# Chunked attention and an MLP block on one core: g broadcast by a product, key transposes in two PSUM banks, fills on GpSimd, other steps for attention

## The chip, the cores and the metric

The kernel runs on one core of a Trainium2 chip. The metric is the device time of one execution in microseconds, median of 11 runs. Engines are named as in the profile: PE is TensorE (matmuls), DVE is VectorE, ACT is ScalarE, POOL is GpSimd, SP is SyncE. SP and POOL issue the DMAs: those that change the type from fp32 to fp16 are on POOL, the stores and the DMA transposes on SP.

## The reference

Two stages follow one another. The first is attention in chunks of 32 queries, each chunk seeing 16 positions to its left, 8 to its right and 8 memory positions; batch 4, 8 heads, 768 positions, head dimension 64:

```
for c in range(nc):                       # chunk of 32 queries
    l_start, r_end = max(0, 32*c - 16), min(S, 32*c + 32 + 8)
    k_full = concat([mem_k, k[:, :, l_start:r_end]])
    v_full = concat([mem_v, v[:, :, l_start:r_end]])
    scores = q_c @ k_full.T / sqrt(D)
    out[:, :, c_start:c_end] = softmax(scores) @ v_full
```

The second is, on x of shape (4, 768, 512), a normalisation and two products with a residual:

```
xn = (x - mu) / sqrt(var + 1e-6) * g_ln
y  = x + relu(xn @ w_ch1) @ w_ch2         # 512 -> 2048 -> 512
```

## The kernel before

**Tiles and units.** The 3072 rows are 24 tiles of 128 rows, six to a batch. Three tiles make a unit, so there are eight units. A unit has 28 steps: steps 0 to 15 are the first product (`up`, one of 16 column blocks per step, four matmuls of 384 columns), steps 16 to 27 the second (`down`, four matmuls of 512 columns per step). The division by the standard deviation is put off to the end: `finish` multiplies by `rstd`, adds x and stores.

**Where attention stands.** Attention for later tiles is spread over these steps. A dictionary `plan`, filled by `at(u, step, fn, ...)`, says which helper is emitted after the product of a step; what is emitted first stands first in the queue of every engine. `attend(i, s0, s1, u)` places one tile: `scores` and the first `soften` at s0, the second at s0 + 1, `values` at s1, `norm` at s1 + 1, `turn_x` and `stats` at s1 + 2. Unit 0 is different: its tiles are attended in a hand-written prologue, with `warm` matmuls on zeros where PE would wait.

**Keys and queries.** A block is 256 positions of k or q. POOL loads it (`load_block`, tile `st`), DVE reorders it (`mix`, `st` to `iv`). For batches 0 and 1 PE transposes it in eight matmuls into PSUM (`turn_block`, L209), and copies bring it to `KT` and `QR`: four `key_piece` copies per key block, alternately on DVE and ACT, and edges from one block to the next (`key_right`, `key_left`). For batches 2 and 3 SP transposes it by DMA (`cross`, L239, `iv` to `rawk` and `QR`), and `spread` copies `rawk` to `KT`. `iv` has four buffers, so the next `mix` waits until a `cross` has read its buffer.

**PSUM.** `att` is two tiles of two banks, `mm` four tiles of one bank; `slot` takes them in turn.

**Fills.** `ones`, `clear_keys` and three memsets put constants into `V` and `KT`, which have two buffers each; `early(1)` does it for batch 1 on DVE at step 15 of unit 0. `v_mem` copies the memory values into `V`, `count_v` corrects the counts in the edge groups. `gb`, g in all 128 partitions, comes by one DMA from POOL.

**The queues.** POOL works in order: loads, then `root` (the standard deviation, waiting on `stats`), then the next loads; batch 3's first loads stand behind the root of tile 11. SP also works in order: `turn_x` of tile 11 is ahead of batch 2's first `cross`.

Of the kernel before, what the change touches and what calls it, by code (L numbers as in the profile page):

```python
# [15 lines left out]
def kernel(  # L16
# [12 lines left out]
    nc = tc.nc  # L29
# [22 lines left out]
    memKT = sb.tile([128, B, 4, 8], FP16, name="memKT")  # L52
    gb = sb.tile([128, 512], FP32, name="gb")
    band = sb.tile([128, 2], FP32, name="band")
    cnt = sb.tile([128, 3], FP32, name="cnt")
# [114 lines left out]

    def key_piece(b, src, g, first, lo, n, eng):

        copy(eng, free(KT[b % 2], GW * g + 16 + 8 * lo, [[W, 4], [8, n], [1, 8]]),
             free(src, 4 * (first + lo), [[1, 4], [4, n], [128, 8]]))

    def key_right(b, g, eng, src=None):

        o = free(KT[b % 2], GW * g + 80, [[W, 4], [1, 8]])
        if src is None:
            copy(eng, o, free(KT[b % 2], GW * (g + 1) + 16, [[W, 4], [1, 8]]))  # L180
        else:
            copy(eng, o, free(src, 0, [[1, 4], [128, 8]]))

# [4 lines left out]

    def keys(b, blk, src, e0, e1):

        g = 4 * blk
        if blk:
            key_right(b, g - 1, e1, src)
        key_piece(b, src, g, 0, 0, 9, e0)
        key_piece(b, src, g + 1, 8, -2, 11, e1)
        key_piece(b, src, g + 2, 16, -2, 11, e0)
        key_piece(b, src, g + 3, 24, -2, 10, e1)
        if blk:
            key_left(b, g, e0)

    def turn_block(b, blk, which, p=None):
        if p is None:
            if (b, blk) not in block_slot:
                block_slot[b, blk] = slot("att")
            p = block_slot[b, blk][:, which, :]
        pv = as16(p)
        i = pick(iv, ("b", b, blk, which))
        for r in range(8):
            nc.tensor.matmul(  # L209
                out=pv[:, 128 * r : 128 * r + 128],  # L210
                lhsT=i[:, 128 * r : 128 * r + 128], rhs=identity,
                is_transpose=True, start=True, stop=True,
            )
        return pv

    block_slot = {}

    def queries(b, blk, pv, e0, e1):
        part_q(b, blk, 0, pv, e0)
        part_q(b, blk, 1, pv, e1)  # L220

    def part_q(b, blk, half, pv, eng):
        copy(eng, free(QR[b % 2], 1024 * blk + 64 * half, [[128, 8], [1, 64]]),
             free(pv, 64 * half, [[128, 8], [1, 64]]))

    def turn_keys(b, blk, e0, e1, *how):
        keys(b, blk, turn_block(b, blk, 0, *how), e0, e1)

    def turn_queries(b, blk, e0, e1, *how):
        queries(b, blk, turn_block(b, blk, 1, *how), e0, e1)  # L230

# [9 lines left out]
    def spread(b, blk, e0, e1):  # L241
        keys(b, blk, pick(rawk, ("b", b, blk)), e0, e1)

# [169 lines left out]

    load_mem_v(0)

    PAIR = 1.0 / 128 + 15.0 / 2**20
# [9 lines left out]

    nc.vector.memset(zero, 0.0)
    ones(0, 0, 2)
    nc.vector.memset(V[0][0:32, 0, :, :], 0.0)
# [4 lines left out]

    load_block(0, 0, 0)
    load_block(0, 0, 1)
    make_identity(nc, identity)

# [5 lines left out]

    total(cnt[:, 0:1], 16, 128)
    total(cnt[:, 1:2], 0, 80)
    total(cnt[:, 2:3], 96, W)
    nc.vector.tensor_tensor(out=cnt[:, 1:2], in0=cnt[:, 1:2], in1=cnt[:, 2:3], op=ALU.add)
    total(band[:, 0:1], 56, 96)
    total(band[:, 1:2], 0, 32)  # L450
    total(cnt[:, 2:3], 88, 96)
    nc.vector.tensor_tensor(out=band[:, 1:2], in0=band[:, 1:2], in1=cnt[:, 2:3], op=ALU.add)
    nc.vector.tensor_scalar(out=band, in0=band, scalar1=NEG, scalar2=None, op0=ALU.mult)

    nc.vector.memset(V[0][64:96, NG - 1, :, :], 0.0)
    load_v(0, 0)
    load_v(0, 1)
    load_block(0, 1, 0)
    nc.gpsimd.dma_start(out=gb, in_=dram(moe_g_ln, 0, [[0, 128], [1, 512]]))
    load_w1(0)  # L460
# [14 lines left out]
    load_v(0, 8)  # L475
    load_v(0, 9)
    load_w2(2)
    load_v(0, 10)
# [6 lines left out]
    mem_vals(0)  # L485
    warm(11)
    mem_keys()
    mem_cols(0, act)
    mix(0, 0, 0, dve)
    pv = turn_block(0, 0, 0, mm[0])  # L490
    key_piece(0, pv, 0, 0, 0, 9, dve)
    key_piece(0, pv, 1, 8, -2, 11, act)
    warm(1)
    mix(0, 0, 1, dve)
    pq = turn_block(0, 0, 1, mm[1])
    part_q(0, 0, 0, pq, act)
    key_piece(0, pv, 2, 16, -2, 11, dve)
    part_q(0, 0, 1, pq, dve)
    warm(1)
    v_mem(0, 0, 2, dve)  # L500
    count_v(0, 0, 0)
    scores(0, 0)
    soften(0, 0, 0)
    soften(0, 0, 1)
    key_piece(0, pv, 3, 24, -2, 10, act)
    warm(2)
    mix(0, 1, 0, dve)
    pv = turn_block(0, 1, 0, mm[2])
    key_right(0, 3, act, pv)
    values(0, 0)  # L510
# [3 lines left out]
    soften(0, 1, 1)  # L514
    ones(0, 2, NG)
    key_piece(0, pv, 4, 0, 0, 9, dve)
    v_mem(0, 2, 6, dve)
    key_piece(0, pv, 5, 8, -2, 11, act)
    warm(2)
    turn_x(0, 0)  # L520
    warm(1)
    up_tile(0, 0, 0, act)
    values(0, 1)
    norm(0, 1)
    key_left(0, 4, dve)
    key_piece(0, pv, 6, 16, -2, 11, dve)
    key_piece(0, pv, 7, 24, -2, 10, act)
    warm(4)
    turn_x(0, 1)
    warm(1)  # L530
    up_tile(0, 0, 1, dve)
    up_tile(0, 1, 0, act)
    up_tile(0, 1, 1, dve)
    mix(0, 1, 1, dve)
    turn_queries(0, 1, dve, act, mm[0])
    warm(1)
    scores(0, 2)
    soften(0, 2, 0)
    soften(0, 2, 1)
    up_tile(0, 2, 0, dve)  # L540
    values(0, 2)
    norm(0, 2)
    up_tile(0, 2, 1, act)
    turn_x(0, 2)
    up_tile(0, 0, 2, dve)
    up_tile(0, 1, 2, act)
    up_tile(0, 2, 2, dve)
    for t in range(3):
        stats(0, t)
    def early(i):  # L550
        ones(i, 0, NG)
        nc.vector.memset(V[i][0:32, 0, :, :], 0.0)
        nc.vector.memset(V[i][64:96, NG - 1, :, :], 0.0)
        clear_keys(i, dve)
        count_v(i, 0, 0)
        count_v(i, 1, NG - 1)

# [17 lines left out]
    for t in range(3):  # L575
        at(0, 16 + t, root, 0, t)
    at(0, 14, v_mem, 0, 6, NG, dve)
    at(0, 14, count_v, 0, 1, NG - 1)
    at(0, 15, early, 1)
    for b in range(1, B):  # L580
        at(0, 14, load_mem_v, b)
        at(0, 23 + b, mem_vals, b)
    at(0, 15, mix, 0, 2, 0, dve)
    at(0, 16, turn_keys, 0, 2, dve, act)
    attend(3, 17, 19, 0)
    at(0, 19, mix, 0, 2, 1, dve)
    at(0, 20, turn_queries, 0, 2, dve, act)
    attend(4, 21, 23, 0)
    attend(5, 22, 24, 0)

# [20 lines left out]
    for b in (1, 2, 3):  # L611
        u = 2 * b - 1
        if b == 1:
            order = [(load_pair, (0,))] + [(load_v, (g,)) for g in range(4)]
            order += [(load_pair, (1,)), (mem_cols, (pool,)), (load_v, (4,)), (load_v, (5,))]
            order += [(load_pair, (2,))] + [(load_v, (g,)) for g in range(6, 12)]
            ahead(1, order, 19, 0.25)
            for blk, s in ((0, (3, 4)), (1, (10, 13)), (2, (24, 25))):
                at(1, s[0] - 1, mix, 1, blk, 0, dve)
                at(1, s[0], turn_keys, 1, blk, dve, act)  # L620
                at(1, s[1] - 1, mix, 1, blk, 1, dve)
                at(1, s[1], turn_queries, 1, blk, act, dve)
            for i in range(3):
                at(1, (4, 12, 19)[i], v_mem, 1, 4 * i, 4 * i + 4, dve)
            attend(6, 5, 9, 1)
            attend(7, 12, 15, 1)
            attend(8, 17, 20, 1)
        else:
            w = u - 1
            at(w, 0, load_pair, b, 0)  # L630
            for i in range(2):
                at(w, 1, load_v, b, i)
            at(w, 2, load_pair, b, 1)
            at(w, 8, mix_pair, b, 0)
            for i in range(2, 4):
                at(w, 9, load_v, b, i)
            at(w, 11, mem_cols, b, pool)
            at(w, 12, mix_pair, b, 1)
            at(w, 13, load_pair, b, 2)
            for i in range(4, 8):  # L640
                at(w, 10 + i, load_v, b, i)
            at(w, 24, mix_pair, b, 2)
            for i in range(8, 12):
                at(w, 13 + i, load_v, b, i)
            at(w, 21, cross_pair, b, 0)
            at(w, 22, cross_pair, b, 1)
            at(u, 3, cross_pair, b, 2)
            at(w, 26, spread, b, 0, dve, act)
            at(w, 27, spread, b, 1, dve, act)
            at(u, 9, spread, b, 2, dve, act)  # L650
            for i in range(3):
                at(w, (17, 20, 23)[i], v_mem, b, 4 * i, 4 * i + 4, dve)
            attend(6 * b, 2, 7, u)
            attend(6 * b + 1, 7, 13, u)
            attend(6 * b + 2, 13, 18, u)
        for i in range(3):
            attend(6 * b + 3 + i, 1 + 6 * i, 6 + 6 * i, u + 1)

# [50 lines left out]
```

## Time and profile before

| | |
|---|---|
| median of 11 runs | 254.59 us (251.08 to 259.15) |
| profiled execution | 257.5 us, span 255.7 us |
| mean granted PE clock | 0.938 |
| PE busy | 221.3 us (87%) |
| DVE busy | 135.0 us (53%) |
| ACT busy | 100.2 us (39%) |
| POOL busy | 96.1 us (38%) |

The span goes from the first to the last instruction; the rest of the profiled execution's time lies around it. In lines of the timeline the columns are start and duration in microseconds, engine, line of the kernel, operation, output and inputs, shapes and count; a bracket at the end gives how long the engine was idle before it and what ended that. In the rows of slices each digit stands for a fortieth of the span, in tenths.

### The profile page before, as it was taken

The page shows a single profiled execution, that of the slowest core. Times are in us where ns is not written, and L with a number is a line of the kernel's source. Part 1 is how long each engine was busy: PE and PEld are TensorE (multiplying, and loading weights), DVE is VectorE, ACT ScalarE, POOL GpSimd, SP SyncE. Part 2 cuts the span into 40 slices and gives each one's busy share as a digit, 9 for nine tenths or more (in the row PEclk, how much of TensorE's full clock was granted, in tenths as well). Part 3 has the DMA queues.
Part 4 walks back from the last instruction along what each step waited for, and adds up shares of the span by engine and source line. Part 5 has one row for each costly group of instructions (what it writes and reads, how often), then busy time and mean ns, then how long its engine had stood idle before and what let it go on. Part 6 is the DMA issues. An engine that isn't in the chain of part 4 may idle for free.

```text
span 255.7 us, 4863 instructions
## 1 busy us (share of the span) xinstructions
PE 221.3 (87%) x1924; PEld 129.9 (51%) x1924; DVE 135.0 (53%) x318; ACT 100.2 (39%) x204; POOL 96.1 (38%) x162
## 2 busy tenths in 40 slices
PE   7578774987798979999238999999999999999994
PEld 2345662443465436654124645664566466546653
DVE  5565456148677644864134843685666426444312
ACT  3521342355356424640216921661478135412300
POOL 8955349996702198129200139532002101110000
PEclk9957998699999999999756999999999999999999
DMA  6999999999961299618995129962963321121012
GB/s 103 146 194 199 200 196 158 154 171 102 183 95 21 64 120 181 60 21 158 132 131 164 23 62 148 173 50 73 204 126 27 81 85 21 23 84 60 3 41 82
DMA packets 72935, 27.59 MB, mean 108 GB/s; under 512 B 60944, under 2 KB 69392, under 8 KB 72912
## 3 DMA queue, kind: packets, MB, share of 16 engines
q0 software_dynamic: 46288, 15.34, 55.2%
q1 hardware_dynamic: 26624, 11.93, 22.1%
q8 instruction: 15, 0.25, 0.4%
q14 instruction: 8, 0.07, 0.1%
HBM read 30.54 MB, written 6.29 MB: 144 GB/s over the span
## 4 chain that ended last, share of the span: by engine, by line
PE 64%; DVE 13%; DMA 10%; issue 3%; ACT 3%; POOL 2%; SPq 2%; DVEq 0%; POOLq 0%; ACTq 0%
PE mm L340 26%; PE mm L366 23%; DMA rawk<-iv 5%; PE att L253 4%; PE att L274 4%; DMA st<-in_k_dram 3%; PE mm L351 3%; DVE xs L282 2%; DVE KT L102 2%; SPq L239 2%; DVE V L102 2%; PE att L209 2%; DVE xn L294 2%; PE mm L388 1%; DMA QR<-iv 1%
## 5 line engine op out<-in xcount | busy, mean ns | idle before, releaser
L340 PE MATMUL mm<-xT,w1c 128*128 128x384 f16 x464 | 84.6, 334 | 5.3 <-DVE rT L334 5.0
L366 PE MATMUL mm<-w2c,rT 128*128 128x512 f16 x368 | 86.0, 386 | 0.0
L340 PEld LDWEIGHTS <-w1c 128*128 128x128 f16 x464 | 51.0, 115 | 29.8 <-issue 8.0
L366 PEld LDWEIGHTS <-rT 128*128 128x128 f16 x368 | 35.1, 99 | 39.6 <-issue 1.9
L332 ACT ACTIVATE rT<-mm 128x384 f16<-128x384 f32 (+1 forms) x62 | 30.5, 495 | 59.9 <-PE mm L340 39.4
L334 DVE TENSOR_SCALAR rT<-mm 128x384 f16<-128x384 f32 (+1 forms) x63 | 35.6, 568 | 30.9 <-PE mm L340 24.0
L305 POOL TENSOR_SCALAR veps<-sq 128x1 f32<-128x1 f32 x24 | 6.9, 286 | 113.0 <-ACT junk L299 112.7
L126 POOL DMA_DIRECT2D V<-in_v_dram x48 | 37.7, 810 | 3.6 <-DMA w2c<-in_moe_w_ch_dram 1.9
L263 ACT ACTIVATE AT<-att,band 104x512 f16<-104x512 f32 x48 | 31.3, 684 | 5.2 <-PE att L253 4.1
L375 DVE SCALAR_TENSOR_TENSOR osb<-mm,rstd,xs 128x512 f32<-128x512 f32 x23 | 17.3, 751 | 26.8 <-PE mm L366 26.8
L299 ACT ACTIVATE junk<-xs,nmean 128x512 f16<-128x512 f32 x24 | 17.2, 718 | 21.5 <-DVE nmean L288 21.4
L253 PE MATMUL att<-QR,KT 64*104 64x64 f16 x384 | 16.3, 237 | 6.2 <-DVE KT L102 5.4
L253 PEld LDWEIGHTS <-KT 64*104 64x104 f16 x384 | 13.3, 138 | 12.5 <-issue 12.2
L100 ACT COPY KT<-rawk 128x352 f16<-128x352 f16 (+2 forms) x16 | 9.4, 651 | 23.3 <-DMA rawk<-iv 23.3
L281 DVE RECIPROCAL rec<-att 128x8 f32<-128x8 f32 x24 | 4.9, 205 | 25.5 <-PE att L274 22.7
L294 DVE SCALAR_TENSOR_TENSOR xn<-xs,nmean,gb 128x512 f16<-128x512 f32 x24 | 17.9, 747 | 0.4
L309 POOL TENSOR_TENSOR rstd<-veps,mhalf 128x1 f32<-128x1 f32 x24 | 16.8, 700 | 2.0
L282 DVE SCALAR_TENSOR_TENSOR xs<-att,rec 128x512 f32<-128x512 f32 x24 | 16.6, 692 | 0.8
L102 DVE COPY iv<-st 128x1024 f16<-128x1024 f16 x24 | 10.2, 440 | 10.4 <-DMA QR<-iv 5.8
L118 POOL DMA_DIRECT2D st<-in_q_dram x24 | 13.6, 581 | 5.4 <-DMA w1c<-in_moe_w_ch_dram 3.7
L118 POOL DMA_DIRECT2D st<-in_k_dram x24 | 13.8, 581 | 3.2 <-DMA w1c<-in_moe_w_ch_dram 2.3
L209 PEld LDWEIGHTS <-iv 128*128 128x128 f16 x96 | 6.2, 105 | 16.8 <-DVE iv L102 16.7
(62 smaller groups left out, 140.0 us busy)
## 6 DMA issues: line engine op xcount, KB each, us to landing
out_dram<-osb SPq DMA_DIRECT2D x23, 256.0 KB, 2.1
V<-in_v_dram POOLq DMA_DIRECT2D x40, 96.0 KB, 5.3
st<-in_k_dram POOLq DMA_DIRECT2D x24, 128.0 KB, 4.8
st<-in_q_dram POOLq DMA_DIRECT2D x24, 128.0 KB, 5.4
w1c<-in_moe_w_ch_dram POOLq DMA_DIRECT2D x4, 512.0 KB, 10.0
w2c<-in_moe_w_ch_dram POOLq DMA_DIRECT2D x4, 512.0 KB, 10.2
V<-in_v_dram POOLq DMA_DIRECT2D x8, 80.0 KB, 5.3
xT<-xn SPq DMA_TRANSPOSE x18, 2.5
```

The lines of the kernel that those rows point to most:

```text
L102: eng.tensor_copy(out=out, in_=in_)
L118: nc.gpsimd.dma_start(out=s[:, 512 * par : 512 * par + 512], in_=dram((k, q)[which], (b * H + 4 * par) * HS + blk * 256 * D, [[512, 32], [ ...
L126: nc.gpsimd.dma_start(out=V[b % 2][lo:hi, g, :, 0:64], in_=dram(v, b * H * HS + (64 * g - 16 + lo) * D, [[64, hi - lo], [HS, H], [1, 64]]),)
L253: nc.tensor.matmul(out=p[0:W, par, (4 * gg + j) * 64 : (4 * gg + j) * 64 + 64], lhsT=KT[b % 2][rows, 2 * t + gg, j, :], rhs=free(QR[b % 2] ...
L263: nc.scalar.activation(out=free(AT[t % 3], 32 * c, [[64, 16], [1, 32]]), in_=free(p, 4 * c, [[64, 16], [1, 4], [8, 8]], W), func=ACTF.Exp, ...
L282: nc.vector.scalar_tensor_tensor(out=x.rearrange("p (h d) -> p h d", h=8), in0=free(p, 0, [[128, 8], [1, 64]]), scalar=1.0, in1=free(r, 0, ...
L294: nc.vector.scalar_tensor_tensor(out=xn[i % 4], in0=xs[i % 9], scalar=nmean[t], in1=gb, op0=ALU.add, op1=ALU.mult,)
L332: nc.scalar.activation(out=o, in_=p, func=ACTF.Relu)
L334: nc.vector.tensor_scalar(out=o, in0=p, scalar1=0.0, scalar2=None, op0=ALU.max)
L340: nc.tensor.matmul(out=p, lhsT=free(w1c[c][:, dt, :], i, [[4, 128]]), rhs=xT[u % 2][:, dt, 128 * lo : 128 * (lo + n)], start=(dt == 0), st ...
L366: nc.tensor.matmul(out=p, lhsT=rT[c][:, k_, 128 * i : 128 * i + 128], rhs=w2c[c][:, k_, :], start=(c == 0 and k_ == 0), stop=(c == 3 and k ...
L375: nc.vector.scalar_tensor_tensor(out=o, in0=p, scalar=rstd[t % 9], in1=xs[t % 9], op0=ALU.mult, op1=ALU.add,)
```

## The change

- g comes as one row of 2 KB on SP (`grow`); a product of a row of ones with it puts it into PSUM in all partitions, and ACT copies it to `gb`.
- Key transposes go into two banks, four matmuls each. `key_piece` takes a half; DVE copies the first bank's half of each piece, ACT the second's. In the prologue the banks are two `mm` tiles, in `turn_keys` the two halves of one `att` tile. The last two pieces are put off (`more_keys`). Queries take a slot of their own and both copies go to ACT.
- `early(1)` moves to POOL and to step 19; other fills, `count_v` and parts of `v_mem` move to other places; the identity is made before the load of q.
- In the prologue the order of copies, ReLUs and tiles changes.
- In unit 1 the steps of keys, queries and attention change. In units 2, 4 and 6 attention starts at steps 0, 5, 10 instead of 1, 7, 13, its values at 5, 10, 15 instead of 6, 12, 18. Of each batch from 2 on the first two blocks' `cross` moves from steps 21 and 22 to 18 and 19, their `spread` from 26 and 27 to 24 and 26.

```diff
-    def key_piece(b, src, g, first, lo, n, eng):
+    def key_piece(b, src, g, first, lo, n, eng, half=None):
+        h, m = (0, 8) if half is None else (4 * half, 4)
+        copy(eng, free(KT[b % 2], GW * g + 16 + 8 * lo + h, [[W, 4], [8, n], [1, m]]),
+             free(src, 4 * (first + lo), [[1, 4], [4, n], [128, m]]))
...
+    PIECES = ((0, 0, 9), (8, -2, 11), (16, -2, 11), (24, -2, 10))
+    def pieces(b, blk, banks, which):
+        for k_ in which:
+            for half, eng in ((0, dve), (1, act)):
+                key_piece(b, banks[half], 4 * blk + k_, *PIECES[k_], eng, half)
...
+    def turn_keys(b, blk):
+        p = slot("att")
+        banks = [as16(p[:, h, :]) for h in range(2)]
+        block_slot[b, blk] = banks
+        transpose_block(b, blk, 0, banks)
+        pieces(b, blk, banks, (0,))
+        if blk:
+            key_right(b, 4 * blk - 1, dve)
+        pieces(b, blk, banks, (1,))
+        if blk:
+            key_left(b, 4 * blk, dve)
+    def more_keys(b, blk):
+        pieces(b, blk, block_slot[b, blk], (2, 3))
+    def turn_queries(b, blk):
+        p = slot("att")
+        pv = as16(p[:, 0, :])
+        transpose_block(b, blk, 1, [pv])
+        part_q(b, blk, 0, pv, act)
+        part_q(b, blk, 1, pv, act)
...
+    nc.sync.dma_start(out=grow, in_=dram(moe_g_ln, 0, [[512, 1], [1, 512]]))
...
     load_block(0, 0, 0)
+    make_identity(nc, identity)
     load_block(0, 0, 1)
-    make_identity(nc, identity)
...
-    nc.gpsimd.dma_start(out=gb, in_=dram(moe_g_ln, 0, [[0, 128], [1, 512]]))
...
-    warm(11)
+    warm(9)
+    p = slot("att")
+    nc.tensor.matmul(out=p[:, 0, :], lhsT=gone, rhs=grow, start=True, stop=True)
+    copy(act, gb, p[:, 0, :])
...
+    K0 = [as16(mm[0]), as16(mm[1])]
+    transpose_block(0, 0, 0, K0)
+    pieces(0, 0, K0, (0, 1))
...
-    ones(0, 2, NG)
-    key_piece(0, pv, 4, 0, 0, 9, dve)
-    v_mem(0, 2, 6, dve)
-    key_piece(0, pv, 5, 8, -2, 11, act)
-    warm(2)
+    warm(3)
     turn_x(0, 0)
+    v_mem(0, 2, 4, dve)
...
     turn_x(0, 1)
-    warm(1)
-    up_tile(0, 0, 1, dve)
-    up_tile(0, 1, 0, act)
-    up_tile(0, 1, 1, dve)
     mix(0, 1, 1, dve)
-    turn_queries(0, 1, dve, act, mm[0])
-    warm(1)
+    warm(1, 512, mm[2])
+    up_tile(0, 0, 1, act)
+    transpose_block(0, 1, 1, [Q0])
+    part_q(0, 1, 0, Q0, act)
+    part_q(0, 1, 1, Q0, act)
+    up_tile(0, 1, 0, dve)
     scores(0, 2)
...
-    at(0, 14, v_mem, 0, 6, NG, dve)
-    at(0, 14, count_v, 0, 1, NG - 1)
-    at(0, 15, early, 1)
+    at(0, 12, v_mem, 0, 6, 8, dve)
+    at(0, 18, v_mem, 0, 8, NG, dve)
+    at(0, 18, count_v, 0, 1, NG - 1)
+            at(0, 19, early, 1, pool)
...
-            for blk, s in ((0, (3, 4)), (1, (10, 13)), (2, (24, 25))):
+            for blk, st_ in ((0, (3, 5)), (1, (9, 12)), (2, (24, 26))):
...
-            attend(6, 5, 9, 1)
-            attend(7, 12, 15, 1)
+            attend(6, 6, 10, 1)
+            attend(7, 13, 16, 1)
...
-            at(w, 21, cross_pair, b, 0)
-            at(w, 22, cross_pair, b, 1)
+            at(w, 18, cross_pair, b, 0)
+            at(w, 19, cross_pair, b, 1)
...
-            at(w, 26, spread, b, 0, dve, act)
-            at(w, 27, spread, b, 1, dve, act)
+            at(w, 24, spread, b, 0, dve, act)
+            at(w, 26, spread, b, 1, dve, act)
...
-            attend(6 * b + 3 + i, 1 + 6 * i, 6 + 6 * i, u + 1)
+            attend(6 * b + 3 + i, 5 * i, 5 + 5 * i, u + 1)
```

## The prediction

> **What bounds the kernel now.** I read the page's 40 slices first, then the timeline of the stretches where the TensorE (PE) digit falls, then DMA and queue lines there.
>
> ```profile
> PE   7578774987798979999238999999999999999994
> PEclk9957998699999999999756999999999999999999
> DMA  6999999999961299618995129962963321121012
> ```
>
> One slice is 6.4 us. Counted from 0, slices 22 on are at 9: matmuls set the end there and only fewer idle microseconds before can shorten the run. Three places are not full: the front (0 to 45 us), unit 1 (64 to 96), and slices 19 to 21 (121 to 140), where PE falls to 2 and 3 and the clock to 7, 5, 6. A unit without holes, such as unit 6 (207.06 to 231.39), takes 24.3 us; unit 1 takes 32.9 (63.6 to 96.5), of which 3.7 are six block transposes, and unit 3 takes 37.0 (120.7 to 157.7).
>
> The timeline of the front's end:
>
> ```profile
> 39.80 1.16 DVE L102 COPY V<-memv 8x3840 f16<-8x3840 f16 x1
> ...
> 41.33 0.70 DVE L420 MEMSET V<- 104x768 f32 x1
> 42.15 0.33 DVE L552 MEMSET V<- 32x320 uint32 x1
> ...
> 43.60 0.41 DVE L102 COPY iv<-st 128x1024 f16<-128x1024 f16 x1
> 44.06 1.03 PE L209 MATMUL att<-identity,iv 128*128 128x128 f16 x8 [3.43 <-DVE iv L102]
> 44.88 1.91 PE L366 MATMUL mm<-w2c,rT 128*128 128x512 f16 x4
> ...
> 50.86 1.04 PE L366 MATMUL mm<-w2c,rT 128*128 128x512 f16 x4
> ```
>
> Fills for two batches stand on VectorE (DVE) ahead of one 0.41 us copy; PE waits 3.43 us and then runs the same four products in 1.91 instead of 1.04 us. The stall at 121 us:
>
> ```profile
> 116.74 1.19 POOL L118 DMA_DIRECT2D st<-in_k_dram  x2
> 116.79 1.30 SPq L239 DMA_TRANSPOSE rawk<-iv  x1
> 118.18 1.73 SPq L239 DMA_TRANSPOSE QR<-iv  x1
> ...
> 119.97 3.35 SPq L239 DMA_TRANSPOSE rawk<-iv  x1
> ...
> 127.19 0.43 DVE L102 COPY iv<-st 128x1024 f16<-128x1024 f16 x1 [4.86 <-DMA QR<-iv]
> ...
> 128.13 0.90 PE L253 MATMUL att<-QR,KT 64*104 64x64 f16 x16 [5.36 <-DVE KT L102]
> ...
> 133.51 0.88 DVE L102 COPY KT<-rawk 128x288 f16<-128x288 f16 x2 [4.44 <-DMA rawk<-iv]
> ...
> 134.99 4.50 PE L340 MATMUL mm<-xT,w1c 128*128 128x384 f16 x16 [4.44 <-DVE rT L334]
> ```
>
> Batch 2's DMA transposes start in the same moment as batch 3's loads. DVE waits in order for two of them (4.86 and 4.44), with the ReLUs behind it, and PE idles 5.36 and 4.44. In unit 5, with no loads beside it, the same transpose lands 3.3 us after issue, not 9.0.
>
> [...] DVE's piece at 68.53 sat idle 0.52 until ScalarE's (ACT) ended. [...] no row here shows a large POOL fill.
>
> **The change, part by part**
>
> *Broadcast of g.* It removes a 256 KB load from POOL's queue (0.57 us of issue, 5.5 to land) and adds a 2 KB load on SP, a product and an ACT copy (0.60, the 128x512 ReLU row). No row shows an fp32 product; I bound it between one warm-up product (0.43) and four (1.7) and take 1.7. Two warm-ups (0.86) go, so the key transposes start up to 0.4 late and ACT about 1.2. Cover: the next key block lands only at 11.73 and starts 11.82 in both. If that cover went, 0.4.
>
> *Keys in two banks.* A piece is now two halves. From DVE's 0.46 at 288 elements and 0.53 at 352, and ACT's 0.45 at 352 and 0.18 at 32, a half costs about 0.32 and 0.29. In the two front blocks the banks are separate tiles and the built program has no wait between the engines: 4 x 0.32 = 1.3 instead of 1.95 in alternation. But the four blocks through turn_keys take both banks from one att tile, and there the program still has each half wait for the other engine's. The chain becomes 4 x 0.32 + 4 x 0.29 + 8 hops of 0.03 + two edges of 0.17 = 3.0, against 1.95 + 3 x 0.03 + 0.17 = 2.2. Behind those waits on DVE stand the ReLUs and the query copy; on ACT the softmax. The change gives a step more room.
>
> *Front order.* Three DVE operations leave the path between the first xn and xT (0.59 + 0.39 + 0.82 = 1.8), but three warm-ups and the half clock take nearly all: xT at 18.1 against 18.19. Key halves then cost 0.6 ahead of the second xT. The query copy moves ahead of two ReLUs, from 27.27 to 24.3, so scores of tile 2 start at 26.9 instead of 28.88; two ReLUs placed ahead of its values give 0.8 back. Its xn is done at 32.05 instead of 33.28. First down product: 1.0 earlier.
>
> *Fills to POOL, v_mem split.* At 39.8 to 43.6 DVE loses everything but 0.6 (count_v and v_mem pieces move to steps where DVE waits for PE). The idle 3.43 goes. With it the half clock from 44 to 51: 0.87 + 0.41 (transposes 1.03 against 0.62) + 0.25 (scores 0.90 against 0.65) + 0.95 (eight downs 2.99 against about 2.04) = 2.5. Late next: the 3.0 us chain and softmax 1.26 end at 44.7, while two downs and scores occupy PE to 43.8: a hole of 0.9; the query transpose then waits 0.7. Net 3.4 + 2.5 - 1.6 = 4.3. On POOL the six fills took DVE 1.74[...]. Behind them are batch 1's loads, issued from 41.3, whose first is used at 66.4: 15 us of cover even with the use 6 us earlier. The identity ahead of q delays q's load by 0.6; DVE used it at 7.70, now at about 8.1.
>
> *Unit 1.* PE idles there now 0.34 + 1.40 + 0.80 + 0.37 + 1.53 = 4.4. Block 0: DVE and ACT halves, one ReLU, the query copy reach 3.0 us after the transposes against two ups (1.5): idle 1.5 for 1.40. Block 1: 1.7 + 0.55 + 1.05 + 1.05 (reciprocal, scale and mean of tile 6, now in between) + 0.42 = 4.6 after overlaps, against 2.5 of PE work: 2.0 for 0.80. Block 2: 3.2 against two downs (2.0): 1.2 for 1.53. Query halves both on ACT (0.58 each) hide behind ups. Together +1.0 us; bounds 0 and +3.
>
> *Attention steps and DMA transposes of units 2 to 6.* Tile 11's values move from step 18 to the end of step 15 (112.50 to 109.7), so its xn is ready at 112.2 instead of 115.52. On SP its transpose is ahead of the moved ones: the first leaves at 113.5 instead of 116.79, and the second pair, behind one store (0.33), at about 116.7 instead of 119.97: 3.3 earlier. But POOL's root of tile 11 also comes earlier, and batch 3's loads stand behind it: 113.8 instead of 116.74, so the collision moves as a whole. With the same landing times from issue (121.8 - 116.8 = 5.0, 127.2 - 118.2 = 9.0, 133.5 - 120.0 = 13.5) DVE is released at 124.0 and 130.3, 3.2 earlier, while PE's downs end at the same point. Against it: spread of block 1 now stands ahead of the last finish, whose PSUM slot the fourth up needs; four ups (0.8) leave the hole. Gain 2.4; bounds 1.0, and 10 if the transposes land as fast as in unit 5. In unit 5 the two small holes (0.18 + 0.59) go: 0.7. PE work added: nothing beside the front.
>
> Sum: -1.0 - 4.3 + 1.0 - 2.4 - 0.7 = -7.4. The profiled execution took 257.5 (span 255.7), 2.9 above the median 254.6 of 11 runs (251.08 to 259.15); it would become 250.1. Taken from the median: 247.2.
>
> **The rivals**
>
> *A, ping-pong keeps more.* The halves on one att tile cost the upper bound in unit 1 (+3) and the stall at 121 us yields only 1.0: -1.0 - 4.3 + 3 - 1.0 - 0.7 = -4.0, 250.6, and down to nothing at 254. For: waits in both directions in the built program, more ACT work. Against: PE has one more step to do.
>
> *B, the stall mostly dissolves.* If the earlier transposes get ahead of the loads in the DMA queues, unit 3 gains 8 instead of 2.4: 247.2 - 5.6 = 241.6. For: 3.3 us uncontended. Against: the loads move by nearly the same, 2.9 us.
>
> *C, slower[...].* If the holes of about 2 us in unit 1, one after each key block, let the clock fall, every microsecond at half clock costs 0.5. In 128 to 139 us the trace shows some 11 us of it after one stall; two such stretches cost 11. It decides when the extra half clock exceeds 2 x 7.4 = 15 us. End: 254.6 - 7.4 + 11 = 258. Against: 1.4 to 1.5 us holes there now leave the clock at 1.00.
>
> *D, it doesn't do what it says:* only two of six key blocks lose the alternation, shown by the waits, and is in the sum.
>
> **How the numbers follow.** About 1% is what a measurement of this kernel can tell from no change. Chances: forecast (244 to 250) 0.52; A 0.24, a third of it within 1% (252.1 to 257.1); B 0.14; C 0.10, mostly beyond 257.1. Faster by over 1%: 0.52 + 0.16 + 0.14 = 0.82, less 0.02 for forecasts that miss: 0.80. Within: 0.11. Slower: 0.09. The range 241 to 253 takes in most of B and A and leaves C out.
>
> **What would show it.** Right: no PE wait of 3 us near 40, first down product near 38.6, unit 1 starting near 58; DVE and ACT key copies alternating in unit 1 with idle times of 0.3; in unit 3 PE still waiting on DVE behind QR<-iv and rawk<-iv, ending 3 us nearer to the unit's start. Wrong: a clock below 9 in slices 10 to 14 (C), no wait on DMA in unit 3 (B), unit 1 over 36 us (A), or the front still bound by a load.

## The result and the profile after

The changed kernel takes 248.25 us (median of 12 runs, 245.13 to 251.14), the kernel before 253.9 (47 runs beside it and beside the experiments, 249.63 to 259.15). The ratio of after to before is 0.9822, 95% interval 0.9783 to 0.9861: 1.8% faster, by more than the 1% that can be told from no change. The ratio leaves out runs more than 1.5% above the fastest of their kernel, as both profiled executions below are, and so lies nearer to 1 than the quotient of the two medians. The forecast was 247.2 (241 to 253).

The profiled execution of the changed kernel took 249.91 us, with a span of 248.1 and a mean granted clock of 0.951 (before: 257.5, 255.7, 0.938). These are three rows of its 40 slices, in tenths, 6.2 us each, counted from 0:

```profile
PE   8797799788769979999129999999999999999994
PEclk9659979999999999999759999999999999999999
DMA  6999999999991399239984139928842211221012
```

Of the three sparse places of before one is smaller: slice 6, which stood at 4, is now at 9. In unit 1 (slices 9 to 14) the clock stays at 9. Slices 19 and 20, in unit 3, are no fuller than before.

The timeline gives the length of each unit: the start of a unit's first `up` matmul (L351, before L340) taken from that of the next unit's. For unit 0, whose `up` part is mixed into the prologue, it is the time from the first `down` (L377, before L366) to unit 1.

| stretch | before | after | difference |
|---|---|---|---|
| front, to the first `down` | 39.61 | 38.49 | -1.1 |
| unit 0, `down` part | 24.18 | 19.24 | -4.9 |
| unit 1 | 32.54 | 33.95 | +1.4 |
| unit 3 | 36.85 | 35.69 | -1.2 |
| unit 5 | 25.06 | 24.09 | -1.0 |
| units 2, 4, 6 together | 73.0 | 72.3 | -0.7 |

The front's end in the timeline of after (start, duration, engine, line, operation; in brackets the idle time before it and what ended that):

```profile
38.49 1.03 PE L377 MATMUL mm<-w2c,rT 128*128 128x512 f16 x4
38.63 0.43 DVE L104 COPY iv<-st 128x1024 f16<-128x1024 f16 x1
...
39.35 0.61 PE L207 MATMUL att<-identity,iv 128*128 128x128 f16 x8
...
40.58 0.75 POOL L569 MEMSET V<- 104x768 f32 x1
...
43.92 1.18 POOL L120 DMA_DIRECT2D st<-in_k_dram  x2
...
44.34 0.44 PE L285 MATMUL att<-V,AT 104*64 104x65 f16 x16 [0.68 <-ACT AT L274]
```

The copy `iv<-st` follows the first `down` at once, the transposes take 0.61 us at full clock, and neither the wait of 3.43 nor the 1.03 us transposes of before are left. The fills lie on POOL from 40.58 to 43.9, ahead of batch 1's loads, and nobody waits for them.

The stall of unit 3 in the same timeline:

```profile
108.72 1.30 SPq L247 DMA_TRANSPOSE rawk<-iv  x1
108.93 1.19 POOL L120 DMA_DIRECT2D st<-in_k_dram  x2
...
112.70 2.74 SPq L247 DMA_TRANSPOSE rawk<-iv  x1
...
118.00 0.43 DVE L104 COPY iv<-st 128x1024 f16<-128x1024 f16 x1 [2.17 <-DMA QR<-iv]
...
118.93 0.65 PE L264 MATMUL att<-QR,KT 64*104 64x64 f16 x16 [1.05 <-DVE KT L104]
...
126.88 0.90 DVE L104 COPY KT<-rawk 128x288 f16<-128x288 f16 x2 [7.67 <-DMA rawk<-iv]
...
128.65 4.79 PE L351 MATMUL mm<-xT,w1c 128*128 128x384 f16 x20 [9.07 <-DVE osb L386]
```

Transposes and batch 3's loads start together again, 0.2 us apart. Block 1's `rawk` is issued at 112.70 and releases DVE at 126.88, 14.2 us later (13.5 before). The two PE waits of 5.36 and 4.44 have become 1.05 and 9.07, in sum 10.1 instead of 9.8. That unit 3 is shorter all the same comes mostly from fewer matmuls at half clock behind the waits: twenty `up` matmuls take 4.79 us here, where sixteen took 4.50.

### The profile page after: what moved, and what is told of

The parts are those of the page before. It is cut to its first block, busy times and chain, and to the rows that moved or that the text cites. A ratio compares the mean times of both kernels' runs of the same rounds, so it can differ in the third digit from the quotient of the medians.

```text
span 248.1 us, 4905 instructions
## 1 busy us (share of the span) xinstructions
PE 218.8 (88%) x1925; PEld 130.7 (53%) x1925; DVE 134.6 (54%) x329; ACT 104.1 (42%) x215; POOL 95.4 (38%) x167
## 4 chain that ended last, share of the span: by engine, by line
PE 54%; DMA 8%; DVE 1%; SPq 0%; issue 0%; ACT 0%; DVEq 0%
PE mm L351 26%; PE mm L377 21%; DMA QR<-iv 5%; PE att L264 3%; DMA rawk<-iv 3%; PE att L285 2%; PE mm L399 1%; DVE osb L386 0%; PE att L207 0%; DVE osb L404 0%; SPq L328 0%; DVE KT L104 0%; ACT KT L102 0%; DVEq L404 0%
## 5 line engine op out<-in xcount | busy, mean ns | idle before, releaser
L351 PE MATMUL mm<-xT,w1c 128*128 128x384 f16 x464 | 82.2, 331 | 9.1 <-DVE osb L386 9.1
L377 PE MATMUL mm<-w2c,rT 128*128 128x512 f16 x368 | 83.7, 379 | 0.0
L351 PEld LDWEIGHTS <-w1c 128*128 128x128 f16 x464 | 51.3, 115 | 32.9 <-issue 10.6
L377 PEld LDWEIGHTS <-rT 128*128 128x128 f16 x368 | 34.6, 98 | 38.8
L345 DVE TENSOR_SCALAR rT<-mm 128x384 f16<-128x384 f32 (+1 forms) x62 | 34.6, 566 | 30.3 <-PE mm L351 23.6
L343 ACT ACTIVATE rT<-mm 128x384 f16<-128x384 f32 (+1 forms) x63 | 31.1, 499 | 43.2 <-PE mm L351 18.7
L310 ACT ACTIVATE junk<-xs,nmean 128x512 f16<-128x512 f32 x24 | 17.3, 721 | 13.5 <-DVE nmean L299 13.4
L102 ACT COPY KT<-rawk 128x352 f16<-128x352 f16 (+1 forms) x12 | 8.8, 791 | 25.4 <-DMA rawk<-iv 25.4
L120 POOL DMA_DIRECT2D st<-in_q_dram x24 | 14.2, 612 | 4.2 <-DMA w1c<-in_moe_w_ch_dram 3.5
L120 POOL DMA_DIRECT2D st<-in_k_dram x24 | 14.3, 611 | 3.2 <-DMA w1c<-in_moe_w_ch_dram 1.8
L320 POOL TENSOR_TENSOR rstd<-veps,mhalf 128x1 f32<-128x1 f32 x24 | 13.4, 557 | 2.0
L285 PEld LDWEIGHTS <-AT 104*64 104x64 f16 x384 | 8.1, 112 | 8.6 <-issue 4.1
## 6 DMA issues: line engine op xcount, KB each, us to landing
w2c<-in_moe_w_ch_dram POOLq DMA_DIRECT2D x4, 512.0 KB, 10.1
```

Of the source, the lines that this page charges most:

```text
L120: nc.gpsimd.dma_start(out=s[:, 512 * par : 512 * par + 512], in_=dram((k, q)[which], (b * H + 4 * par) * HS + blk * 256 * D, [[512, 32], [ ...
L310: nc.scalar.activation(out=junk, in_=xs[(NT * b + t) % 9], func=ACTF.Square, bias=nmean[t], scale=1.0, accum_out=sq[t],)
L343: nc.scalar.activation(out=o, in_=p, func=ACTF.Relu)
L345: nc.vector.tensor_scalar(out=o, in0=p, scalar1=0.0, scalar2=None, op0=ALU.max)
L351: nc.tensor.matmul(out=p, lhsT=free(w1c[c][:, dt, :], i, [[4, 128]]), rhs=xT[u % 2][:, dt, 128 * lo : 128 * (lo + n)], start=(dt == 0), st ...
L377: nc.tensor.matmul(out=p, lhsT=rT[c][:, k_, 128 * i : 128 * i + 128], rhs=w2c[c][:, k_, :], start=(c == 0 and k_ == 0), stop=(c == 3 and k ...
```

## The experiments

In each, "unit" times are read as in the table above.

**The changed kernel once more**, for a second profiled execution, without an edit.

> The changed kernel itself, unchanged, as the base of the three runs beside it on this chip: 247 to 250, with one hole of 7 to 10 us in unit 3.

Median 249.44 (244.73 to 250.9, 4 runs), beside 253.37 for the kernel before on the same chip. The profiled execution is the fastest, 244.73. Two of its rows of slices:

```profile
PE   7577797976879889998079999999999999999994
PEclk9999999999999999999559999999999999999999
```

The front runs at full clock here, with the first `down` at 34.17 instead of 38.49; unit 0 (19.3), unit 1 (34.1) and the stall are much as they were (unit 3: 34.7). The last products ahead of the first full `up` show the clock by their time, in the first execution and in this one:

```profile
31.58 4.47 PE L362 MATMUL mm<-xT,w1c 128*128 128x128 f16 x48 [0.58 <-DVE xT L338]
```

```profile
28.89 2.84 PE L362 MATMUL mm<-xT,w1c 128*128 128x128 f16 x48 [0.58 <-DVE xT L338]
```

So one kernel's front differs by 4.3 us from one execution to the next, which no step of the prediction had reckoned with.

**Batch 3's first loads later**, on the changed kernel. Behind the root of tile 12 instead of that of tile 11, POOL issues them when the transposes are over.

```diff
-            at(w, 0, load_pair, b, 0)
+            late = 3 if b == 3 else 0
+            at(w, late, load_pair, b, 0)
...
-                at(w, 1, load_v, b, i)
-            at(w, 2, load_pair, b, 1)
+                at(w, max(1, late), load_v, b, i)
+            at(w, max(2, late), load_pair, b, 1)
```

> The changed kernel with batch 3's first loads (two blocks of k and q, two of v) moved on POOL from behind the root of tile 11 to behind the root of tile 12. Theory 1, contention: batch 2's DMA transposes are slow only because these loads run beside them. Then they land about 3.3 us after issue as in unit 5, the hole of 9.07 us in unit 3 shrinks to under 2, the half clock after it goes, unit 3 falls from 35.9 us to 25 to 27 and the median to about 239. Theory 2, the transposes hold each other up in their own queue: landing stays 8 to 14 us from issue, unit 3 stays over 33, the median over 246.

236.54 us (234.53 to 237.0, 4 runs), ratio 0.9355 (0.9265 to 0.9444). Its rows of slices, 5.8 us each:

```profile
PE   7587698878759969999999999999999999999994
PEclk9999999999999999999999999999999999999999
```

And its timeline in unit 3, the SP and the POOL queue:

```profile
104.94 1.30 SPq L247 DMA_TRANSPOSE rawk<-iv  x1
...
108.31 1.29 SPq L247 DMA_TRANSPOSE rawk<-iv  x1
...
123.92 1.19 POOL L120 DMA_DIRECT2D st<-in_k_dram  x2
```

The loads leave at 123.92, 15 us behind the transposes. A transpose holds SP for 1.3 us and not for 2.7, DVE waits for none, and unit 3 takes 24.1 us (112.00 to 136.11) without one hole. The collision of loads and transposes is what makes the stall, and in unit 3 it is worth about 11 us in the changed kernel (35.7 and 34.7 in its two executions, 24.1 here). The 11.7 by which the medians differ need not all be this: the granted clock is 1.00 in all four runs here, so their fronts ran at full clock too.

**The same edit on the kernel before.**

> The kernel before with the same loads moved. Theory 1, contention: unit 3 falls from 36.9 us to 26 to 28 (the transposes leave 3.3 us later than in the changed kernel, so a hole of 1 to 2 us may stay), the median from 254 to about 245. Theory 2: unit 3 over 34, median over 251. The distance to the run before this one is then what the rest of the change is worth: 5 to 6 us.

246.35 us (244.99 to 247.65), ratio 0.976 (0.9646 to 0.9874). Unit 3 takes 25.9 us (120.52 to 146.38), while the wait of 3.42 us near 44 stays. The cause is the same in both kernels. The distance of this kernel to the last one is 9.8 us, not the 5 to 6 expected. In the profiled executions, whose spans differ by 11.6, unit 0 gives 5.1, unit 3 1.7 and the front 5.3, since it ran at half clock here (first `down` at 39.75) and at full clock there (34.48); unit 1 takes 2.1 back, and units 2, 4, 5 and 6 give the other 1.6.

**The move of the fills alone**, on the kernel before.

```diff
-    def early(i):
+    def early(i, eng):
...
-    at(0, 14, v_mem, 0, 6, NG, dve)
-    at(0, 14, count_v, 0, 1, NG - 1)
-    at(0, 15, early, 1)
+    at(0, 12, v_mem, 0, 6, 8, dve)
+    at(0, 18, v_mem, 0, 8, NG, dve)
+    at(0, 18, count_v, 0, 1, NG - 1)
+    at(0, 26, count_v, 1, 0, 0)
+    at(0, 26, count_v, 1, 1, NG - 1)
...
+            at(0, 19, early, 1, pool)
```

> The kernel before with the move of the fills alone: batch 1's memsets on POOL at step 19 of unit 0, v_mem and count_v of batch 0 split to steps 12 and 18 as in the changed kernel. Theory 1: the PE wait of 3.43 us at 40 us goes and the half clock after it too, 5 to 6 us together, median about 249. Theory 2, the half clock has another cause: 3 us, median about 251. Theory 3, POOL's memsets delay batch 1's loads onto the path: no gain.

247.65 us (247.31 to 250.81), ratio 0.9838 (0.9728 to 0.9949). TensorE in its timeline where before had the wait:

```profile
39.22 1.03 PE L366 MATMUL mm<-w2c,rT 128*128 128x512 f16 x4
40.08 0.61 PE L209 MATMUL att<-identity,iv 128*128 128x128 f16 x8
40.53 1.03 PE L366 MATMUL mm<-w2c,rT 128*128 128x512 f16 x4
```

The `down` part of unit 0 takes 18.6 us instead of 24.2. This part alone gives as much as the whole change within the intervals.

**The attention, transpose and spread steps of units 2 to 6 put back**, on the changed kernel.

```diff
-            at(w, 18, cross_pair, b, 0)
-            at(w, 19, cross_pair, b, 1)
+            at(w, 21, cross_pair, b, 0)
+            at(w, 22, cross_pair, b, 1)
...
-            at(w, 24, spread, b, 0, dve, act)
-            at(w, 26, spread, b, 1, dve, act)
+            at(w, 26, spread, b, 0, dve, act)
+            at(w, 27, spread, b, 1, dve, act)
...
-                attend(6 * b + 3 + i, 5 * i, 5 + 5 * i, u + 1)
+                attend(6 * b + 3 + i, 1 + 6 * i, 6 + 6 * i, u + 1)
```

> The changed kernel with the steps of attention, DMA transposes and spread in units 2 to 6 put back to those before. Theory 1, as the two profiles stand: unit 3 1 us longer and unit 5 1 us longer, median about 250.3. Theory 2, as the prediction had it: 3.1 us longer, 251.4. Theory 3, the whole collision moves with its deadline and nothing is won: 248.3.

248.99 us (245.18 to 253.1), ratio 0.9798 (0.9666 to 0.9929): no difference to the changed kernel that the runs could tell. Units 2, 4 and 6 are 0.24 us longer each and unit 5 1.2, as the old steps would have it. But unit 3 takes 32.7 us, three less than after: block 1's `rawk`, issued at 114.83, releases DVE at 123.60, after 8.8 us.

```profile
123.60 0.88 DVE L104 COPY KT<-rawk 128x288 f16<-128x288 f16 x2 [1.13 <-DMA rawk<-iv]
```

**The spread of block 1 at step 27 again**, alone.

```diff
-            at(w, 26, spread, b, 1, dve, act)
+            at(w, 27, spread, b, 1, dve, act)
```

> The changed kernel with the spread of each second block moved one step back, behind the last finish of the unit (step 27, as before the change). The prediction priced the order at 0.8 us: four ups stand in the hole of unit 3 again instead of behind it. Theory 1: PE waits twice there, with four ups between, and the median is 0.5 to 1 us lower, 247.5. Theory 2, the order of the two on DVE also held the next store and transposes on SP back and so helped the landing: no gain or up to 2 us slower.

248.1 us (246.93 to 249.62), ratio 0.9832 (0.974 to 0.9924). Unit 3 takes 34.4 us, against 35.7 and 34.7 in the two executions of the changed kernel; four `up` matmuls stand in the hole again, ahead of a wait of 6.56. The 0.8 us in question isn't resolved, by the times or by one profile.

**Keys of batch 1's first two blocks in two separate tiles** of `mm` instead of the two halves of one `att` tile.

```diff
-        p = slot("att")
-        banks = [as16(p[:, h, :]) for h in range(2)]
+        if b == 1 and blk < 2:
+            banks = [as16(slot("mm")) for h in range(2)]
+        else:
+            p = slot("att")
+            banks = [as16(p[:, h, :]) for h in range(2)]
```

> The changed kernel with the first two key blocks of batch 1 transposed into two single-bank mm tiles instead of the two banks of one att tile, so that no half waits for the other engine's. Theory 1, the alternation makes the holes of 1.53 and 1.67 us in unit 1: the key copies of an engine follow one another without idle time, the two holes shrink by about 1 us each, unit 1 falls from 34.0 to about 32 us and the median to about 246.5. Theory 2, the query copy and the mean of tile 6 on DVE make the holes: they stay over 1.2 us and the median stays at 248.

247.26 us (246.47 to 250.2), ratio 0.9768 (0.9679 to 0.9857); unit 1 takes 32.4 us instead of 34.0. The key copies of one block in the timeline of the changed kernel, DVE and ACT:

```profile
69.49 0.31 DVE L104 COPY KT<-att 128x144 f16<-128x144 f16 x1 [0.78 <-PE att L207]
...
70.59 0.31 ACT L102 COPY KT<-att 128x176 f16<-128x176 f16 x1 [0.48 <-DVE KT L104]
...
71.73 0.32 DVE L104 COPY KT<-att 128x160 f16<-128x160 f16 x1 [0.37 <-ACT KT L102]
```

The same block in the run with separate tiles:

```profile
66.86 0.31 DVE L104 COPY KT<-mm 128x144 f16<-128x144 f16 x1 [0.49 <-PE mm L207]
...
67.08 0.89 ACT L102 COPY KT<-mm 128x144 f16<-128x144 f16 x4 [0.59 <-PE mm L207]
...
68.28 0.56 DVE L104 COPY KT<-mm 128x176 f16<-128x176 f16 x2
```

In one tile each half waits for the other engine's, and the last DVE half ends 2.6 us after the first one began. In two tiles ACT's four pieces run in one go and DVE's end after 2.0 us, edges included. Behind them on DVE stands the `mix` for which PE's query transposes wait. The lines of these transposes for the first two blocks, in the kernel before, the changed kernel and this run:

```profile
69.56 0.61 PE L209 MATMUL att<-identity,iv 128*128 128x128 f16 x8 [1.40 <-ACT KT L100]
...
79.25 0.62 PE L209 MATMUL att<-identity,iv 128*128 128x128 f16 x8 [0.80 <-DVE iv L102]
```

```profile
64.28 0.62 PE L207 MATMUL att<-identity,iv 128*128 128x128 f16 x8 [1.53 <-DVE iv L104]
...
73.50 0.62 PE L207 MATMUL att<-identity,iv 128*128 128x128 f16 x8 [1.67 <-DVE iv L104]
```

```profile
61.95 0.62 PE L207 MATMUL att<-identity,iv 128*128 128x128 f16 x8 [0.81 <-DVE iv L104]
...
70.29 0.62 PE L207 MATMUL att<-identity,iv 128*128 128x128 f16 x8 [0.58 <-DVE iv L104]
```

The 1.6 us is shown in the unit, not in the times of the whole run, whose spread is 4 us.

**g by the DMA of before**, on the changed kernel.

```diff
-    nc.sync.dma_start(out=grow, in_=dram(moe_g_ln, 0, [[512, 1], [1, 512]]))
+    nc.gpsimd.dma_start(out=gb, in_=dram(moe_g_ln, 0, [[0, 128], [1, 512]]))
...
-    warm(9)
-    p = slot("att")
-    nc.tensor.matmul(out=p[:, 0, :], lhsT=gone, rhs=grow, start=True, stop=True)
-    copy(act, gb, p[:, 0, :])
+    warm(11)
+    slot("att")
```

> The changed kernel with g loaded in all partitions by one DMA on POOL behind the key block again, two warm-ups back in place of the fp32 product, no ACT copy. Theory 1: the next key block's landing covers both forms, 0 to 0.4 us either way, 248.3. Theory 2, POOL's issue and 256 KB in the full DMA queues delay the first loads: 0.5 to 1.5 us slower, above 249.

247.8 us (245.93 to 250.94), ratio 0.9775 (0.968 to 0.987), first `down` at 34.61, against 34.17 and 34.48 in the two executions with the product whose fronts ran at full clock. The way in which g is spread makes no difference that these runs can tell.

**Both edits that gained in their unit**: the later loads and the keys in separate tiles.

> The changed kernel with both edits that showed a gain in their unit: batch 3's first loads issued at step 3 of unit 4 (as in the run with the loads later) and batch 1's first two blocks of keys in two separate PSUM tiles. Theory 1 (the two gains lie in different units, 3 and 1, and add): unit 3 near 24.1 us, unit 1 near 32.4, median 236.5 - 1.7 = about 234.8. Theory 2 (what unit 1 gains is taken by the next wait, because the PE is full from there on only when it starts where it did): unit 1 shorter but unit 2 or 3 longer by as much, median 236.5.

236.7 us (235.12 to 237.31), ratio 0.9437 (0.9362 to 0.9512), so no better than the later loads alone. The profiled execution (span 234.7, against 232.8) says where the gain went. Unit 1 is 2.1 us shorter (32.35 against 34.47), but the front is 2.7 longer (first `down` at 37.15, part of it at half clock), and there is a new hole at the start of unit 4:

```profile
138.05 0.81 PE L354 MATMUL mm<-xT,w1c 128*128 128x384 f16 x4 [1.28 <-DMA xT<-xn]
```

+2.7 - 2.1 + 1.3 is the 1.9 by which the spans differ. The transpose for which the hole waits leaves at 131.48 among the loads that were moved, and lands after 6.4 us; in the run with the later loads alone it left at 130.94 among the same loads, landed after 5.0, and PE waited for nothing. Whether the hole belongs to the kernel or to this execution, one profile of each doesn't tell; nor is the front's clock an effect of the edit that these runs show. Expected was that the gains add (234.8); the median is that of the other theory, but its shift to the next wait is only seen in part. The two kernels are equal within the interval, and both beat the changed kernel by some 12 us.

**The kernel before once more**, for a second profiled execution, without an edit.

> The kernel before itself, for a second profiled execution. Theory 1 (the front's clock and the landing of block 1's queries differ between executions of one kernel): first down product anywhere from 35 to 39.6 us and the idle time of unit 3 anywhere from 5 to 10 us, the median 254. Theory 2 (both belong to the kernel): first down product at 39.6 and two holes of about 5 us in unit 3 again.

253.88 us (251.66 to 254.88). From its timeline in unit 3:

```profile
120.74 2.99 SPq L239 DMA_TRANSPOSE rawk<-iv  x1
...
130.28 0.87 DVE L102 COPY KT<-rawk 128x288 f16<-128x288 f16 x2 [1.99 <-DMA rawk<-iv]
```

Block 1's `rawk` releases DVE 9.5 us after issue, not 13.5, and unit 3 takes 33.0 us, not 36.9. So the landing varies by 4 us from execution to execution of one kernel. The front is at half clock again, first `down` at 40.63: of the two things expected to vary, here the landing did and the front by only 1.0 us.

**More warm-up products in the kernel before**: six instead of two, which fill TensorE's wait near 11 us.

```diff
-    warm(2)
+    warm(6)
     mix(0, 1, 0, dve)
```

> The kernel before with six warm-up products instead of two ahead of the mix of block 1, which fills the idle PE time near 11 to 12 us. Theory 1 (the half clock of the front follows from gaps of PE work just ahead of it): the clock stays full in the front, first down product near 35.5 instead of 39.6, median near 250. Theory 2 (the half clock has another cause than that gap): first down stays at 39.5 or later by up to 1 us, median 253.9 to 255.

253.5 us (251.16 to 254.6), ratio 1.0105 (1.0002 to 1.0207). The clock from 12 to 16 us is 1.00 instead of 0.63, but from 16 to 20 it is 0.56, behind waits of 0.93 and 1.99 us that were not filled, and the first `down` comes at 40.71. In this execution the fall has moved, not gone.

**These waits filled too.**

```diff
-    warm(2)
+    warm(6)
     turn_x(0, 0)
-    warm(1)
+    warm(9)
     up_tile(0, 0, 0, act)
```

> The run with six warm-up products on the kernel before moved the fall of the clock from 12 to 17 us, behind the next two gaps of 0.93 and 1.99 us. Here these are filled too: six warm-up products instead of two ahead of the first xT, nine instead of one behind it. Theory 1 (how full PE is just before decides the clock): full clock through 20 us, first down product at 35 to 36.5 instead of 40.7, median about 4 below the kernel before. Theory 2 (the fall comes whatever stands in the gaps): half clock again before 22 us, first down at 40 or later, median 0 to 2 above the kernel before.

253.91 us (250.79 to 254.2), ratio 1.0121 (0.9928 to 1.0315). The clock in the slices of the two runs, this one first; a slice is 6.3 us:

```profile
PEclk9999997799999999999756999999999999999999
```

and the one with only the first gap filled:

```profile
PEclk9986979599999999999977999999999999999999
```

Now the front keeps its full clock to the end of the prologue (what is left is the fall behind the 3.35 us wait near 42), and the first `down` starts at 37.46, 3.2 us earlier than in the kernel before seen again, though later than the 35 to 36.5 expected. That is what the first theory has for the clock, in one execution; it isn't shown that the filling did it, since the changed kernel's front ran at full clock beside unfilled waits of up to 1.4 us, and the mean clocks of the four runs here (0.959 to 0.977) lie within those of the kernel before beside them (0.932 to 0.977). And the time of the run didn't follow. In the profiled execution unit 3 took 35.7 us instead of 33.0 and gave 2.7 of the 3.2 back. Whether an earlier arrival there causes the longer stall, or the landing only happened to be late, these runs don't tell.

## Why the prediction was right, and where its steps were not

The direction, the size and the main cause were right; one step, unit 3, came to nothing, and another, the front, was too small, which partly made up for it.

**Fills (-4.3).** Right, and shown by itself: -4.9 in the changed kernel, -5.6 with this part alone. The new holes were forecast at 0.9 and 0.7 and measured 0.68 and 0.73. POOL needed 3.3 us for the fills, for which DVE had needed 1.74, and as forecast nobody waited for that. The holes were in the sum; the transposes and `down`s at half clock went together with the wait of 3.43 us (transposes 0.61 instead of 1.03, both in the changed kernel and with this part alone).

**Unit 1 (+1.0, bounds 0 and 3).** Right in kind: 33.9 to 34.5 us, +1.4 to +1.9, in six executions with the keys in one tile. The PE waits behind the three blocks were forecast at 1.5, 2.0 and 1.2 and are 1.53, 1.67 and 1.35. That the alternation is the cause is shown by the keys in separate tiles, where 1.6 to 2.1 us go. The waits of the halves on each other are 0.37 on DVE and 0.4 to 0.5 on ACT. The part of rival D that stood in the sum, that only two of six blocks lose the alternation, is thereby confirmed. What isn't separated in that edit is that it also leaves an `att` tile free for other work.

**Front (-1.0).** -1.1 in the first pair of profiles, but that agreement is luck. In eight profiled executions with the changed front (one with g by DMA) the first `down` came between 34.17 and 38.49, mean 36.3; in four with the front of before between 39.22 and 40.63, mean 39.8. The difference of the means is -3.5. It may be too large, since five of the eight took less time than any other run of their kernel. The failing term is "three warm-ups and the half clock take nearly all": the half clock of 12 to 20 us was taken over from the profile of before as if it belonged to the work. In three of the eight executions (first `down` at 34.2 to 34.6) nothing behind the opening warm-ups runs at half clock. In the other five the 48 products shown above take 4.2 to 4.5 us instead of 2.84, and four of these five have half clock between 5 and 18 us too. None of the four of before was free of it. At full clock the gain is there: the first `up_tile` starts at 15.57 in the changed kernel's second execution and at 17.12 in the kernel before with its waits filled, so that some 1.5 of the 1.8 us that left the path are kept. (The row of the clock seems to begin only with a trace's first change: with the steps put back it reads full from the start, while eight transposes at 7.48 take 1.03 us instead of 0.62.) g's broadcast at no cost was right: the product took 1.12 us where the clock was full, inside the bounds of 0.43 and 1.7.

**Unit 3 (-2.4, bounds 1.0 and 10).** This step failed at "with the same landing times from issue". Against the start of unit 3 the first `rawk` was issued 3.2 us earlier than before, as forecast, and block 1's 2.4 (forecast 3.3). Against the same start DVE was released by `QR` 4.3 us earlier, but by block 1's `rawk`, which came last, only 1.7 instead of 3.2. The landing time isn't a property of the transpose: in these executions it runs from 8.8 to 14.2 us. From issue to DVE's release:

| steps of units 2 to 6 | landing of block 1's `rawk`, us | unit 3, us |
|---|---|---|
| old (before twice, both warm-up runs, fills alone, steps put back) | 13.5, 9.5, 9.6, 10.6, 12.9, 8.8; mean 10.8 | 36.9, 33.0, 33.0, 35.7, 36.4, 32.7; mean 34.6 |
| new (after twice, spread at 27, keys in two tiles, g by DMA) | 14.2, 13.0, 13.4, 13.0, 14.0; mean 13.5 | 35.7, 34.7, 34.4, 35.5, 35.8; mean 35.2 |

Block 1's transpose left 2.4 us earlier and took 2.7 longer. By these means the moved steps gained nothing in unit 3 that the executions show. Why it takes longer with the new steps is not settled: a store stands between the two pairs, and `rawk` of block 1 leaves 3.5 to 4.1 us behind the first load, with more loads ahead of it, where it was 3.1 to 3.4 in most executions with the old steps; but one of these had 4.1 and landed after 10.6. The gain of 1.2 in the first pair of profiles is small beside the 4 us by which unit 3 differs among the executions with the old steps.

**Unit 5 (-0.7)** measured -1.0, and units 2, 4 and 6 gave 0.24 each that weren't in the sum; the run with the steps put back loses both.

**The sum.** The forecast had -7.4, from 257.5 to 250.1; the profiled pair gave -7.6. Against the medians it overshot: 253.9 - 248.25 = 5.65. The base was 0.7 too high (254.59 of 11 runs, where 47 gave 253.9), which made up part of it; hence 248.25 for 247.2. The means of the stretches over all profiled executions add up to about -8, so 2 us more than the medians show; they can't be placed better with executions that differ by 4 us in the front and by 4 in unit 3.

**The rivals.** A (250.6) was nearer in unit 3, where it gave 1.0, and too dear in unit 1, which took +1.4 to +1.9 of its +3. B falls in its condition: the stall stayed in all executions with the loads where they were; that it was worth 10 us and more is shown by moving the loads. C falls: the clock in unit 1 is 1.00 beside waits of 1.5 us.

## What to carry to other kernels

When a stall begins as two groups of DMAs start in the same moment, look for the instruction that issues the second group and move it behind the first; here that was a change of three step numbers, worth some 11 us in the changed kernel's unit 3 and 7.6 in the median of the kernel before, where the whole larger change gave 5.7. A landing time read beside other traffic is no constant to add to a new start: block 1's `rawk` took 8.8 to 14.2 us in the executions here that have the loads beside it. Take a second profiled execution before a microsecond of difference in a sparse stretch is put down to an edit.

## What was not expected of the hardware

- TensorE's clock fell to half (0.50 granted) in a sparse front without a wait like the 3.43 us ahead of the half clock at 44 in the kernel before. In the profiled execution of the changed kernel the fall comes with the transposes at 8.65, behind a wait of 1.24:

```profile
6.58 0.62 PE L207 MATMUL mm<-identity,iv 128*128 128x128 f16 x8
...
8.65 1.03 PE L207 MATMUL mm<-identity,iv 128*128 128x128 f16 x8 [1.24 <-DVE iv L104]
```

  In the second execution of the same kernel it didn't fall there, behind a wait of 0.83, nor behind one of 1.14 at 19.11, and in unit 1 of the first it stayed at 1.00 beside waits of 1.53 and 1.67. So in these executions the length of the last wait alone doesn't decide it; what does isn't shown. In the first profiled execution of each kernel the time between two changes of the granted clock is a whole multiple of 3.41 us: the half clock lasts 10.2, 6.8 and 13.7 us in the kernel before and 10.2, 3.4 and 10.2 in the changed one. With the waits filled in the kernel before the clock stayed up, and with two left unfilled the fall came behind these, in one execution each.
- One fp32 product of 128x512 with a single row of weights counts as two matmuls of together 1.12 to 1.14 us at full clock (2.07 in two executions whose front was still at half clock, 1.46 in a third). At full clock each further fp16 warm-up product of the same size adds 0.22: three take 0.82, four 1.04.
- A DMA transpose holds SP for 1.3 us in the run with the loads later, and block 1's two hold it for 1.8 to 6.0 us each in the eleven executions that have loads beside them, so that what stands behind them on SP leaves late too: in the changed kernel the second was issued at 115.53, held SP for 4.36, and the store behind it left at 119.99.
